# Where the sorting of batch 3's keys sits among the second dense layers of batch 2

## The chip, the cores and the metric

The kernel runs on one NeuronCore of a Trainium2 chip. The metric is the device time of one execution in microseconds (us), lower is better; each kernel is run several times and the median is compared.

The engines of the core each work through their own list of instructions in order. TensorE (PE) multiplies matrices and writes its results to PSUM; VectorE (DVE) and ScalarE (ACT) take results out of PSUM and compute on them; GpSimd (POOL) and SyncE (SP) here mostly start transfers (DMAs). An engine waits for another by a semaphore. "PEld" in the profile is TensorE's loading of the stationary operand, which can overlap its multiplying.

## The reference

For 4 batches of 8 heads, 768 positions and head size 64, a small 8x8 matrix per head is normalised five times over rows and columns (`P`). The 8 blocks (of 96 positions) of the keys and of the values are mixed with it, each block of queries attends to its mixed block, and the result goes through a two-layer dense network:

```python
k_sorted = np.einsum('bhij,bhjcd->bhicd', P, k_b)     # "sorting" the keys
v_sorted = np.einsum('bhij,bhjcd->bhicd', P, v_b)     # and the values
scores = scale * np.matmul(q_b, k_sb.transpose(0, 1, 2, 4, 3))
attn = softmax(scores)                                # within one block
x = np.matmul(attn, v_sb)                             # 3072 tokens x 512
h = x @ w_in                                          # 512 -> 2048
r = np.maximum(h, 0.0)
out = (s * (r * r) + b) @ w_out                       # 2048 -> 512
```

## The kernel before

The work is cut into 8 tiles `t` of 384 tokens, two per batch (`t` = 2b and 2b+1). A tile passes through these pieces:

- `k_piece(b, c0, nc2, nb, eng)` (multiplied at L294) sorts a part of a batch's keys. The pieces of this text, `K(3, c0, 16, eng)`, load 16 pairs of key columns from `kb` one after the other as the stationary operand, multiply each with the mixing matrix into one PSUM buffer `tk`, and copy this to `ks` with four casts, on DVE (`eng` "v", L238) or ACT (`eng` "s", L240). Three pieces with `c0` = 0, 32, 64 make a batch.
- `S2(t, hp)` is two calls of `s_piece`: scores (L375) into PSUM buffers `sc`, and their exponentials on ACT into `at` (L378). It needs the sorted keys `ks` of its batch.
- `P2(t, hp)` is two calls of `p_piece`: attention times sorted values `vs` (L402) into PSUM buffers `pv`, then a reciprocal and a multiplication on DVE into `x` (L406, L407).
- `T(t)` is `x_turn`: a transposing DMA on SP's queue from `x` to `xt` (L452).
- `ffn1(t)` (L473) multiplies by `w_in`; ACT takes the positive part (L477) and DVE squares it into `gt` (L478).
- `ffn2(t)` (L516) multiplies by `w_out`: three row groups of 16 matmuls into a PSUM buffer `ops`; DVE scales it, adds the bias (L490) and SP stores it (L492).

All orders are written by hand: the program's order is each engine's order. To fill TensorE's list evenly, `ffn1` and `ffn2` take a `Queue` of attention pieces for later tiles. `ffn2` calls the queue after every fourth matmul, so `ffn2(2)` and `ffn2(3)` together have 24 slots, numbered 0 to 23 below; the queue of the change has 24 entries, one per slot (`nothing` is an empty one).

PSUM is given out in turn from two pools. The one that matters here, `psa`, has three buffers, used in rotation by `tk`, `sc`, `pv` and `hps` (the result of `ffn1`). A piece that takes a buffer waits until its last reader has finished.

Ahead of this queue, POOL starts the transfers of batch 2 and 3 (L664 to L668), once the queries of batch 2 have been transposed:

```python
nc.gpsimd.tensor_copy(out=gate2, in_=QT[2][0:1, NHP - 1, S - 1:S])
v_read(2, nc.gpsimd)       # sorted values of batch 2, two DMAs (vs<-dv, L361)
load_k(*brows(3))          # keys of batch 3, one DMA (kb<-in_k_dram, L97)
v_read(3, nc.gpsimd)       # sorted values of batch 3, two DMAs
load_q(3)                  # queries of batch 3, six DMAs (L84)
```

Slot 22 of the queue, `q_turn(3)`, transposes those queries on SP's queue. The sorted keys and the turned queries of batch 3 are first read by `S2(6, 0)`, in `ffn2(4)`, after `ffn1(4)` and `ffn1(5)`.

Of the kernel before, what the change touches and what calls it, by code (L numbers as in the profile page):

```python
# [18 lines left out]
def kernel(  # L19
# [58 lines left out]
    def load_q(b, part=slice(0, 128)):  # L78


        if b > 1:
            qr[b] = qrp.tile([128, TQ, H, D], BF, tag="qr", name=f"qr{b}")
            for t in range(TQ):
                nc.gpsimd.dma_start(  # L84
                    out=qr[b][:, t],
                    in_=q[b][:, t * 128:(t + 1) * 128, :].rearrange("h p d -> p h d"))
            return
        if b not in qr:
            qr[b] = qrp.tile([128, H, TQ, D], BF, tag="qr", name=f"qr{b}")
        nc.gpsimd.dma_start(  # L90
            out=qr[b][part].rearrange("p h t d -> p h (t d)"),
            in_=q[b].rearrange("h (p t) d -> p h (t d)", t=TQ)[part])

    def load_k(rows, prow, n=1):
        for c0 in range(0, BLK, BLK // n):
            cs = slice(c0, c0 + BLK // n)
            nc.gpsimd.dma_start(out=kb[prow, cs, :], in_=kraw[rows, cs, :])  # L97
# [4 lines left out]
    def brows(b):  # L102
        return slice(b * 64, (b + 1) * 64), slice((b % 2) * 64, (b % 2) * 64 + 64)
# [157 lines left out]
    def q_piece(b, hp0, eng):  # L261

        if hp0 == 0:
            QT[b] = qtp.tile([128, NHP, S], BF, tag="qt", name=f"qt{b}")
        ps = psa.tile([128, 2, 1024], BF, tag="a", name="tq")
        for i in range(2):
            for t in range(TQ):
                for e in range(2):
                    nc.tensor.transpose(
                        out=ps[e * 64:(e + 1) * 64, i, t * 128:(t + 1) * 128],  # L270
                        in_=qr[b][:, 2 * (hp0 + i) + e, t, :], identity=ident)
        evac(QT[b][:, hp0:hp0 + 2, :].rearrange("q a (p t) -> q a p t", t=TQ),
             ps[:, :, 0:S].rearrange("q a (t p) -> q a p t", t=TQ), eng)

    def q_turn(b):

        QT[b] = qtp.tile([128, NHP, S], BF, tag="qt", name=f"qt{b}")
        for t in range(TQ):
            nc.sync.dma_start(out=QT[b][:, :, t * 128:(t + 1) * 128],
                              in_=qr[b][:, t].rearrange("p h d -> p (h d)"), transpose=True)  # L280

    def k_piece(b, c0, nc2, nb, eng):

        pr = brows(b)[1] if nb == 1 else slice(0, 128)
        rhs = (pd1[pr] if b < 2 else pd2[pr, b - 2]).rearrange("p e m i -> p (e m i)")
        if nc2 * nb > 8:
            ps = psa.tile([128, nc2, nb * 64], FP, tag="a", name="tk")  # L290
        else:
            ps = psb.tile([128, nc2, nb * 64], FP, tag="b", name="tk")
        for c in range(nc2):
            nc.tensor.matmul(out=ps[:, c, :],  # L294
                             lhsT=kb[pr, c0 + 2 * c:c0 + 2 * c + 2, :].rearrange("p c d -> p (c d)"),
                             rhs=rhs, start=True, stop=True)
        g0 = (b % 2) * 32

        def half(cp):
            if b == 0:  # L300
                cs = slice(c0 + cp, c0 + 2 * nc2, 2)
            else:
                cs = slice(cp * (BLK // 2) + c0 // 2, cp * (BLK // 2) + c0 // 2 + nc2)
            for e in range(2):
                evac(ks[e * 64:(e + 1) * 64, g0:g0 + nb * 32, cs].rearrange(
                         "p (b g) c -> p b g c", b=nb),
                     ps[cp * 64:(cp + 1) * 64].rearrange(
                         "p c (b e g) -> p e b g c", b=nb, e=2)[:, e], eng)

        half(0)  # L310
        return lambda: half(1)
# [54 lines left out]
    def s_piece(t, hp):  # L366

        b, half = divmod(t, 2)
        g0 = (b % 2) * 32 + hp * NB + half * HB
        sc = psa.tile([BLK, 2, 512], FP, tag="a", name="sc")  # L370
        for n in range(HB):
            for e in range(2):
                pr = slice(e * 64, (e + 1) * 64)
                q0 = (half * HB + n) * BLK
                nc.tensor.matmul(out=sc[:, e, n * BLK:(n + 1) * BLK], lhsT=ks[pr, g0 + n, :],  # L375
                                 rhs=QT[b][pr, hp, q0:q0 + BLK], start=True, stop=True)
        at = atp.tile([BLK, 2, TG], BF, tag="at", name="at")
        nc.scalar.activation(out=at, in_=sc[:, :, 0:TG], func=AF.Exp, scale=scale)  # L378
        AT[t, hp] = at

    def p_piece(t, hp, n0=0, nn=HB):

        b, half = divmod(t, 2)
        at = AT[t, hp]
        if t not in X:
            X[t] = xp.tile([BLK, HB, d_model], BF, tag="x", name="x")
        x = X[t]
        atf = at.rearrange("p e t -> p (e t)")
        if nn < HB:
            p1 = psb.tile([128, 512], FP, tag="b", name="pv")  # L390
            pv = [p1[:, e * nn * VW:(e + 1) * nn * VW] for e in range(2)]
            pvv = p1[0:BLK, 0:2 * nn * VW].rearrange("p (e n w) -> p e n w", e=2, w=VW)
        else:
            p2 = psa.tile([128, 2, 512], FP, tag="a", name="pv")
            pv = [p2[:, 0], p2[:, 1]]
            pvv = p2[0:BLK, :, 0:nn * VW].rearrange("p e (n w) -> p e n w", w=VW)
        for e in range(2):
            for n in range(n0, n0 + nn):
                c0 = (e * HB + n) * BLK
                m = 128 if c0 + 128 <= 2 * TG else BLK  # L400
                gi = e * 32 + hp * NB + half * HB + n
                nc.tensor.matmul(out=pv[e][0:m, (n - n0) * VW:(n - n0 + 1) * VW],  # L402
                                 lhsT=atf[:, c0:c0 + m],
                                 rhs=VS[b][:, gi, :], start=True, stop=True)
        rec = rtp.tile([BLK, 2, HB], FP, tag="rec", name="rec")
        nc.vector.reciprocal(out=rec[:, :, 0:nn], in_=pvv[:, :, :, D])  # L406
        nc.vector.tensor_tensor(  # L407
            out=x[:, n0:n0 + nn, hp * 128:(hp + 1) * 128].rearrange("p n (e d) -> p e n d", e=2),
            in0=pvv[:, :, :, 0:D],
            in1=rec[:, :, 0:nn].unsqueeze(3).broadcast_to([BLK, 2, nn, D]), op=ALU.mult)  # L410
# [38 lines left out]
    def x_turn(t):  # L449

        XT[t] = xtp.tile([128, HB * NHP, BLK], BF, tag="xt", name="xt")
        nc.sync.dma_start(out=XT[t], in_=X[t].rearrange("p n m -> p (n m)"), transpose=True)  # L452
# [87 lines left out]
    def seq(*fs):  # L540
        def run():
            for f in fs:
                f()
        return run

    def S2(t, hp):
        return lambda: (s_piece(t, hp), s_piece(t, hp + 1))

    def P2(t, hp):
        return lambda: (p_piece(t, hp), p_piece(t, hp + 1))  # L550

    def T(t):
        return lambda: x_turn(t)

    def attn(t):
        return [S2(t, 0), nothing, P2(t, 0), S2(t, 2), nothing, P2(t, 2), nothing, T(t)]
# [77 lines left out]
    def csums(f0, f1):  # L634
        for f in range(f0, f1):
            if f == 1:
                nc.gpsimd.tensor_tensor(out=csum, in0=wo_at(0), in1=wo_at(1), op=ALU.add)
            elif f > 1:
# [9 lines left out]
    qu = Queue([nothing, lambda: q_piece(1, 2, "v")]  # L648
               + [lambda c0=c0: k_piece(1, c0, 16, 1, "vsv"[c0 // 32])() for c0 in range(0, BLK, 32)]
               + [seq(lambda: load_q(2), lambda: load_k(*brows(2)), bias_piece), V2[0], S2(2, 0), V2[1], S2(2, 2), V2[2], V2[3],  # L650
                  P2(2, 0), V2[4], P2(2, 2), V2[5], S2(3, 0),
                  T(2), P2(3, 0), S2(3, 2), nothing, P2(3, 2), T(3), lambda: q_turn(2)], 24)
# [3 lines left out]
    def K(b, c0, nc2, eng):  # L656
        return lambda: k_piece(b, c0, nc2, 1, eng)()

    qu = Queue([nothing if i % 2 else K(2, i * 8, 8, "vs"[i // 2 % 2]) for i in range(12)]
               + [nothing] * 4, 16)  # L660
# [5 lines left out]
    load_k(*brows(3))  # L666
    v_read(3, nc.gpsimd)
    load_q(3)  # L668
    qu = Queue([S2(4, 0), K(3, 0, 16, "s"), nothing, P2(4, 0), nothing, S2(4, 2), nothing,
                K(3, 32, 16, "s"), P2(4, 2), nothing, T(4), K(3, 64, 16, "v"), S2(5, 0), nothing,  # L670
                nothing, P2(5, 0), nothing, S2(5, 2), nothing, P2(5, 2), nothing, T(5),
                lambda: q_turn(3), nothing], 24)
    ffn2(2, qu)
    ffn2(3, qu)
# [2 lines left out]
    qu = Queue(attn(6) + attn(7), 24)  # L677
# [36 lines left out]
```

## Time and profile before

| | |
|---|---|
| time, median of 13 runs | 237.28 us |
| lowest and highest of these runs | 236.15 and 238.92 us |
| the profiled execution's own time | 238.71 us |
| span of the profile | 237.0 us |
| mean granted TensorE clock | 0.964 |
| TensorE busy with matmuls | 226.9 us, 96% of the span |
| VectorE, ScalarE, GpSimd busy | 121.9, 111.9, 48.4 us |

The profile shows one execution; its times count from the start of its span. The busy share of an engine is an average over stages. Which stage is held up by what is read from the waits, and from the list of instructions in order of time. The granted clock is the share of full speed at which TensorE was allowed to run.

### The profile page before, as it was taken

Reading aid. Unit: us, or ns where it says so; the run is one execution under the profiler, and the core shown is the slowest. Engines: PE = TensorE matmul, PEld = TensorE weight load, DVE = VectorE, ACT = ScalarE, POOL = GpSimd, SP = SyncE. Lnnn points to the kernel's source line nnn. Section 1 sums busy time; section 2 is a strip of 40 time slices with the busy share of each in tenths; the row PEclk is TensorE's granted clock in tenths of the full one; section 3 lists DMA queues with packets and bytes.
Section 4 is the critical chain, followed back from the end, with each engine's and each line's share of the span. In section 5 each row is a group of like instructions: output and inputs, shape, how many; then the busy total and the mean of one; then the engine's idle time right before and its main releaser. Section 6 shows DMA issues by size and latency. Waiting matters only on the chain.

```text
span 237.0 us, 4847 instructions
## 1 busy us (share of the span) xinstructions
PE 226.9 (96%) x2036; PEld 137.3 (58%) x2036; DVE 121.9 (51%) x257; ACT 111.9 (47%) x164; POOL 48.4 (20%) x62
## 2 busy tenths in 40 slices
PE   8969999999999999999789999999999999999994
PEld 5769897765544555555345455665554556554442
DVE  4768556638992646666322745434352544342221
ACT  6158479675157451778635321566422225660000
POOL 7820000399991000059210000000000000000000
PEclk9975599999999999999979999999999999999999
DMA  5799999998699995539999815630024142001122
GB/s 91 116 203 211 230 192 205 228 225 177 88 117 182 297 273 131 121 62 123 156 104 162 173 44 117 86 89 1 3 85 103 58 116 39 3 0 44 59 77 89
DMA packets 46694, 28.90 MB, mean 122 GB/s; under 512 B 35920, under 2 KB 41040, under 8 KB 46160
## 3 DMA queue, kind: packets, MB, share of 16 engines
q0 software_dynamic: 18800, 15.21, 49.1%
q1 hardware_dynamic: 27728, 13.32, 24.5%
q8 instruction: 16, 0.26, 0.5%
q10 hardware_dynamic: 144, 0.07, 0.1%
q14 instruction: 6, 0.05, 0.1%
HBM read 29.63 MB, written 8.65 MB: 162 GB/s over the span
## 4 chain that ended last, share of the span: by engine, by line
PE 63%; issue 15%; DMA 10%; POOL 8%; ACT 2%; DVE 0%; POOLq 0%
PE hps L473 25%; PE ops L516 25%; DMA kb<-in_k_dram 5%; DMA qr<-in_q_dram 5%; POOL csum L639 4%; PE pv L402 3%; PE sc L375 2%; POOL qr L84 2%; PE tv L320 2%; PE ops L501 1%; ACT ks L240 1%; PE wp L182 1%; PE tq L254 1%; PE tk L294 1%; PE tv L336 1%
## 5 line engine op out<-in xcount | busy, mean ns | idle before, releaser
L473 PE MATMUL hps<-xt,wi 128*128 128x384 bf16 (+1 forms) x576 | 88.1, 309 | 0.3 <-ACT rt L477 0.3
L516 PE MATMUL ops<-wo,gt 128*128 128x512 bf16 x368 | 87.8, 383 | 0.4 <-DVE ot L490 0.4
L477 ACT ACTIVATE rt<-hps 128x768 bf16<-128x768 f32 (+1 forms) x72 | 53.2, 741 | 45.0 <-PE hps L473 44.2
L473 PEld LDWEIGHTS <-wi 128*128 128x128 bf16 x576 | 53.7, 98 | 30.3 <-issue 1.3
L478 DVE TENSOR_TENSOR gt<-rt 128x768 bf16<-128x768 bf16 (+1 forms) x72 | 41.2, 575 | 47.1 <-ACT rt L477 46.7
L516 PEld LDWEIGHTS <-gt 128*128 128x128 bf16 x368 | 34.1, 99 | 38.2 <-issue 2.0
L490 DVE SCALAR_TENSOR_TENSOR ot<-ops,s_bc,bias 128x512 f32<-128x512 f32 x23 | 17.1, 749 | 44.4 <-PE ops L516 44.3
L378 ACT ACTIVATE at<-sc 96x768 bf16<-96x768 f32 x32 | 24.4, 804 | 29.2 <-PE sc L375 29.1
L407 DVE TENSOR_TENSOR x<-pv,rec 96x512 bf16<-96x512 f32 (+1 forms) x36 | 22.6, 627 | 1.3
L240 ACT CAST ks<-tk 64x512 bf16<-64x512 f32 (+1 forms) x32 | 16.0, 501 | 8.6 <-PE tk L294 8.3
L238 DVE CAST ks<-tk 64x512 bf16<-64x512 f32 (+1 forms) x32 | 18.1, 565 | 2.0 <-PE tk L294 1.5
L639 POOL TENSOR_TENSOR csum<-csum,wo 128x512 f32<-128x512 f32 x14 | 17.6, 1255 | 1.0
L402 PEld LDWEIGHTS <-at 96*128 96x128 bf16 (+1 forms) x256 | 12.5, 106 | 4.1 <-issue 0.6
L182 PE MATMUL wp<-zt 128*128 128x256 bf16 x86 | 13.4, 319 | 1.1 <-DVE warm L113 1.1
L402 PE MATMUL pv<-vs,at 96*128 96x66 bf16 (+1 forms) x256 | 13.4, 202 | 0.1
L240 ACT CAST vn<-tv 128x512 bf16<-128x512 f32 (+1 forms) x12 | 9.4, 799 | 7.2 <-PE tv L350 6.7
L375 PEld LDWEIGHTS <-ks 64*96 64x96 bf16 x256 | 8.5, 128 | 5.8 <-issue 5.1
L84 POOL DMA_DIRECT2D qr<-in_q_dram x12 | 10.6, 912 | 5.4 <-DMA kb<-in_k_dram 3.0
L406 DVE RECIPROCAL rec<-pv 96x8 f32<-96x8 f32 (+1 forms) x36 | 6.9, 192 | 8.7 <-PE pv L402 8.6
L182 PEld LDWEIGHTS <-zt 128*128 128x128 bf16 x86 | 9.2, 113 | 2.9 <-DVE warm L113 1.1
L375 PE MATMUL sc<-qt,ks 64*96 64x96 bf16 x256 | 10.8, 219 | 0.0
L294 PEld LDWEIGHTS <-kb 64*128 64x128 bf16 x192 | 6.7, 98 | 6.7 <-issue 4.0
(73 smaller groups left out, 98.8 us busy)
## 6 DMA issues: line engine op xcount, KB each, us to landing
out_dram<-ot SPq DMA_DIRECT2D x23, 256.0 KB, 2.3
kb<-in_k_dram POOLq DMA_DIRECT2D x4, 768.0 KB, 11.8
vb<-in_v_dram POOLq DMA_DIRECT2D x4, 768.0 KB, 19.8
wi<-in_moe_w_in_dram POOLq DMA_DIRECT2D x2, 1024.0 KB, 20.2
wo<-in_moe_w_out_dram POOLq DMA_DIRECT2D x2, 1024.0 KB, 32.5
qr<-in_q_dram POOLq DMA_DIRECT2D x12, 128.0 KB, 9.9
dv<-vn SPq DMA_DIRECT2D x6, 256.0 KB, 7.6
vs<-dv POOLq DMA_DIRECT2D x4, 384.0 KB, 13.2
```

Of the source, the lines that this page charges most:

```text
L182: nc.tensor.matmul(out=wp, lhsT=zt[:, 0:128], rhs=zt, start=True, stop=True)
L238: nc.vector.tensor_copy(out=out, in_=in_)
L240: nc.scalar.copy(out=out, in_=in_)
L375: nc.tensor.matmul(out=sc[:, e, n * BLK:(n + 1) * BLK], lhsT=ks[pr, g0 + n, :], rhs=QT[b][pr, hp, q0:q0 + BLK], start=True, stop=True)
L378: nc.scalar.activation(out=at, in_=sc[:, :, 0:TG], func=AF.Exp, scale=scale)
L402: nc.tensor.matmul(out=pv[e][0:m, (n - n0) * VW:(n - n0 + 1) * VW], lhsT=atf[:, c0:c0 + m], rhs=VS[b][:, gi, :], start=True, stop=True)
L407: nc.vector.tensor_tensor(out=x[:, n0:n0 + nn, hp * 128:(hp + 1) * 128].rearrange("p n (e d) -> p e n d", e=2), in0=pvv[:, :, :, 0:D], in1 ...
L473: nc.tensor.matmul(out=hps[:, f, 0:nt], lhsT=wi_at(hp, f0 + f), rhs=xt_at(t, hp, n0, nn), start=(hp == 0), stop=(hp == NHP - 1))
L477: nc.scalar.activation(out=rt[:, :, 0:nt], in_=hps[:, :, 0:nt], func=AF.Relu)
L478: nc.vector.tensor_tensor(out=gt[:, f0:f0 + 2, c0:c0 + nt], in0=rt[:, :, 0:nt], in1=rt[:, :, 0:nt], op=ALU.mult)
L516: nc.tensor.matmul(out=ops, lhsT=gt[:, f, m * 128:(m + 1) * 128], rhs=wo_at(f), start=(f == 0), stop=(f == NF - 1))
L639: nc.gpsimd.tensor_tensor(out=csum, in0=csum, in1=wo_at(f), op=ALU.add)
```

## The change

The three pieces that sort batch 3's keys leave slots 1, 7 and 11 and go to slots 11, 14 and 20 of the same queue. The piece in slot 11 is still evacuated by VectorE, the two others by ScalarE. All other entries keep their slots.

```diff
-    qu = Queue([S2(4, 0), K(3, 0, 16, "s"), nothing, P2(4, 0), nothing, S2(4, 2), nothing,
-                K(3, 32, 16, "s"), P2(4, 2), nothing, T(4), K(3, 64, 16, "v"), S2(5, 0), nothing,
-                nothing, P2(5, 0), nothing, S2(5, 2), nothing, P2(5, 2), nothing, T(5),
+    qu = Queue([S2(4, 0), nothing, nothing, P2(4, 0), nothing, S2(4, 2), nothing, nothing,
+                P2(4, 2), nothing, T(4), K(3, 0, 16, "v"), S2(5, 0), nothing, K(3, 32, 16, "s"),
+                P2(5, 0), nothing, S2(5, 2), nothing, P2(5, 2), K(3, 64, 16, "s"), T(5),
                 lambda: q_turn(3), nothing], 24)
```

## The prediction, made before the changed kernel was run

> **What bounds the kernel now.** I read the page first: the span, the busy times, the slices.
>
> ```profile
> span 237.0 us, 4847 instructions
> PE 226.9 (96%) x2036; PEld 137.3 (58%) x2036; DVE 121.9 (51%) x257; ACT 111.9 (47%) x164; POOL 48.4 (20%) x62
> PE   8969999999999999999789999999999999999994
> PEclk9975599999999999999979999999999999999999
> ```
>
> TensorE bounds it: no other engine is busy for much over half of the span. A slice is 5.9 us. Apart from the start and the end, the PE row is below 9 only in slices 19 and 20 (112.6 to 124.4 us), and the clock row is below 9 after the start only in slice 20. This is the stage of the edited queue. I then asked for TensorE's waits. From 30 to 117 us they come to 0.7 us, from 126 us to the end to none. For 98 to 150 us they are:
>
> ```profile
> PEld L294 <- DMA kb<-in_k_dram: 2.7, 1, 2.7
> PE tk L294 <- DMA kb<-in_k_dram: 2.2, 1, 2.2
> ```
>
> Columns: total, times, longest. One wait of 2.2 us, for the keys of batch 3, by the first matmul of `K(3, 0)`. The timeline shows what it follows and what stands behind it:
>
> ```profile
> 115.68 0.56 PE L375 MATMUL sc<-qt,ks 64*96 64x96 bf16 x16
> 116.17 1.04 PE L516 MATMUL ops<-wo,gt 128*128 128x512 bf16 x4
> 119.39 0.64 PE L294 MATMUL tk<-pd,kb 64*128 64x64 bf16 x16 [2.19 <-DMA kb<-in_k_dram]
> 119.96 2.60 PE L516 MATMUL ops<-wo,gt 128*128 128x512 bf16 x8
> 122.35 1.14 PE L402 MATMUL pv<-vs,at 96*128 96x66 bf16 x16
> ```
>
> Slot 0 (`S2(4, 0)`), four dense matmuls, then the wait in slot 1; everything in later slots is queued behind it. The stage table shows a second price, the granted clock (after the engines, before the DMA share):
>
> ```profile
> 118.00:119.00 1.00, 0.00 (x0) 0.00 (x0) 0.00 (x0) 0.00 (x0) 0.00 (x0) 1.00 1.02 107
> 121.00:122.00 1.00, 1.00 (x4) 0.38 (x3) 0.00 (x0) 0.98 (x3) 0.00 (x0) 0.51 0.94 86
> 123.00:124.00 1.00, 1.00 (x11) 0.58 (x9) 0.97 (x3) 0.00 (x0) 0.00 (x0) 0.50 1.12 127
> 124.00:125.00 1.00, 1.00 (x5) 0.41 (x4) 0.97 (x3) 0.00 (x0) 0.00 (x0) 0.78 2.84 111
> ```
>
> From 121.0 to 124.4 us, just after the idle stretch, TensorE ran at half clock. The chain of waits, in order of time, gives what that cost:
>
> ```profile
> 119.39 0.64 PE tk L294 x16
> 120.03 2.53 PE ops L516 x8
> 122.56 0.93 PE pv L402 x16
> 123.49 2.26 PE ops L516 x8
> 125.75 0.49 PE sc L375 x16
> 126.23 1.83 PE ops L516 x8
> 128.07 0.57 PE tk L294 x16
> ...
> 129.61 0.54 PE pv L402 x16
> ```
>
> The same pieces at full clock follow in the list: 8 dense matmuls 1.83 us, a `P2` 0.54 us.
>
> **The change, step by step.**
>
> *Removed: the wait.* The keys were asked for at 106.56 us and landed 12.8 us later, at 119.35 us. Their first user moves from slot 1 (about 117.2 us) to slot 11, which I place below at 127.6 us: 8.2 us of slack. Gain 2.19 us, and 0.07 us for the slow first piece (0.64 against 0.57).
>
> *Removed: the half clock, if the idle stretch caused it.* (2.53 - 1.83) + (0.93 - 0.54) + (2.26 - 1.83) = 1.52 us. [...] The trace speaks otherwise: half clock for 3.4 us right behind that gap, none anywhere else after the first 30 us, though equal key pieces without a wait run at 128 and 132.7 us. I take the trace: 1.52 us for the profiled execution. [...]
>
> *Moved: three key pieces.* Each is 16 weight loads, 16 matmuls and four casts, and issues no DMA; POOL's and SP's lists keep their order, and nothing is moved past a transfer. TensorE's work is the same: three times 0.57 us. The number of places where dense matmuls are interrupted stays 11 too. The piece in slot 11 stays VectorE's; its four casts (2.78 us) are there before and after, so VectorE's list is unchanged. ScalarE's two groups of casts (2.35 us each) move from behind the exponentials of slots 0 and 5 to behind those of slots 12 and 17.
>
> *The stage rebuilt.* With the chain's pieces from 116.17 us: 12 dense matmuls 2.70, `P2` 0.54, 8 dense 1.83, `S2` 0.49, 12 dense 2.70, `P2` 0.54, 12 dense 2.59: slot 11 at 127.56. Then key piece 0.57, 4 dense 0.97, `S2` 0.49, 8 dense 1.83, key piece 0.57, 4 dense 0.97, `P2` 0.54, 8 dense 1.73, `S2` 0.49, 8 dense 1.83, `P2` 0.53, 4 dense 0.97, key piece 0.57, 12 dense 2.59: `ffn1(4)` begins at 142.2 instead of 146.03 us, 3.8 us earlier. Step by step it was 2.19 + 0.07 + 1.52 = 3.8. Both agree.
>
> *What is late next.* `P2(4, 0)` in slot 3 is now the first to need a transfer, at 116.17 + 2.70 = 118.9 us. The two transfers of batch 2's values were started at 103.85 and 105.22 us. The transfer table has the first alone, then both (median of two):
>
> ```profile
> vs<-dv POOLq DMA_DIRECT2D x1, 384.0 KB, 7.7
> ...
> vs<-dv POOLq DMA_DIRECT2D x2, 384.0 KB, 9.0
> ```
>
> So the second took 2 x 9.0 - 7.7 = 10.3 us and landed at 115.5 us, 3.4 us ahead of need. It is started before the keys on the same queue and landed 3.8 us before them: an execution with slower transfers delays both. The exponentials that `P2(4, 0)` needs end at 117.6 us. No wait: 0.
>
> *New tight places*, all on the rotation of three PSUM buffers. The piece in slot 14 takes the buffer of the piece in slot 11: VectorE finished that 3.48 us after its first matmul (132.74 to 136.22 in the timeline of before), TensorE comes back 3.86 us after it (0.57 + 0.97 + 0.49 + 1.83). Margin 0.4 us; if a delay eats it, TensorE waits that much, say up to 0.5 us. `S2(5, 2)` at 135.2 needs the slot-14 buffer, whose casts end at 131.4 + 0.67 + 2.35 = 134.4: margin 0.8. The last casts begin 0.67 us after 139.05 and end at 142.1, while ScalarE is needed by the first result of `ffn1(4)` at 142.2 + 1.34 = 143.5: margin 1.5, and the shortfall beyond it would be the cost. Together 0, bounds -0.1 and +0.8. The sorted keys are first read at 168.5 - 3.8 = 164.7 us, over 22 us later. The transposed queries too: their last transfer was issued at 119.63, the six had a median of 17.6 us to landing, and the transposes go at about 142 us; should they wait, SP's list waits with them, with the first store of `ffn2(3)`'s last rows behind, not TensorE.
>
> *After the stage.* From 126 us on TensorE has no wait; what is won here is kept to the end. Tail and start are untouched.
>
> *Sum.* 238.71 - 3.8 = 234.9 us for the profiled execution. It lay 1.43 us above the median. If that excess is the half clock, the median run loses 2.2 us only, and 237.28 - 2.2 = 235.1 results: the same place. If the excess came from the start, the median run gains all of it: 237.28 - 3.8 = 233.5 us. I take 234.9.
>
> **The rivals.**
>
> *The half clock stays* (about one in eight): it has another cause, or another short gap brings it. Then 2.3 us are won: 238.71 - 2.3 = 236.4 on the profiled execution, 235.0 from the median. [...] Against it: the place of the dip.
>
> *The wait is mostly moved, or typical runs hardly have it* (about one in twelve): the lowest run, 236.15, is 2.56 us below the profiled one, so some executions may have little to win; with the tight PSUM places costing 0.8, 236.2 to 238. Against: then another 2.5 us of variation would have to sit at the start.
>
> *Slower: TensorE waits for batch 2's values in slot 3* (one in twenty). The wait decides the other way if those land 2 us after need, at 120.9 instead of 115.5: 234.9 + 2.0 + 1.5 for a half-clock stretch = 238.4, 0.5% above the median; at 3 us, 239.4. For it: this is the first transfer met[...]. Against it: in the trace the keys come 3.8 us behind the values, so a run with the values 2 us late for slot 3 would have had the keys at 124.8 us, a wait of some 7.6 us in the kernel before, and no run was beyond 238.92.
>
> *The change does nothing* (within the second rival): excluded as far as order goes, since TensorE's list differs only in these 48 matmuls and their weight loads.
>
> **How the numbers follow.** Full gain 0.75, half clock stays 0.12, little or none 0.08, slower 0.05. About 0.5% (1.2 us) is what a measurement of this kernel can tell from no change: faster means below 236.1 us. The first case and nearly all of the second lie there, 0.87; the third is the same, 0.08; the last slower, 0.05. The range goes from the full gain off the median, 233.5 and a tenth, to the second rival's 236.4.
>
> **What would show it.** Right: no TensorE wait on `kb`, no granted clock below 1.00 between 30 us and the end, slot 3's `P2` at about 118.9 us, the first `ffn1(4)` matmul 26.0 us after the end of slot 0's scores instead of 29.9. Wrong: a wait of the first `pv` matmul for `vs`, of `tk` or `sc` for DVE or ACT of a microsecond, or a half-clock stretch that remains without the gap.

## The result, and the profile after

The changed kernel took 235.02 us (median of 11 runs, 234.56 to 235.20). The kernel before, its new runs pooled with the earlier ones, took 237.71 us (48 runs, 236.00 to 239.06). The ratio is 0.9886, 95% interval 0.9861 to 0.9911: 1.1% faster. Forecast were 234.9 us and 233.4 to 236.4.

The profiled execution after took 235.37 us with a span of 233.7 us. Its page, the lines that answer to those of before:

```profile
span 233.7 us, 4849 instructions
PE 225.8 (97%) x2036; PEld 137.1 (59%) x2036; DVE 122.0 (52%) x257; ACT 111.9 (48%) x164; POOL 48.4 (21%) x62
PE   8969999999999999999999999999999999999994
PEclk9995599999999999999999999999999999999999
```

The dent in slices 19 and 20 is gone from the PE row, and the 7 in slice 20 from the clock row; VectorE, ScalarE and GpSimd are busy as long as before to 0.1 us; TensorE's busy time falls by 1.1 us: about 1.5 us less here, where its matmuls no longer run at half clock, and about 0.5 us more at the start (see below). TensorE's waits from 30 us to the end are now:

```profile
PE ops L516 <- DVE ot L490: 0.4, 1, 0.4
PE hps L473 <- ACT rt L477: 0.3, 1, 0.3
```

The wait for `kb` is not in the list. These two were there before. The chain of waits, in order of time (start, duration), through the edited queue:

```profile
116.31 0.49 PE sc L375 x16
116.80 2.70 PE ops L516 x12
119.50 0.53 PE pv L402 x16
120.03 1.73 PE ops L516 x8
...
125.48 2.59 PE ops L516 x12
128.07 0.57 PE tk L294 x16
...
131.93 0.57 PE tk L294 x16
...
139.46 0.57 PE tk L294 x16
140.03 2.70 PE ops L516 x12
142.72 5.36 PE hps L473 x33
```

It is TensorE all the way, each piece at its full-clock duration. From the end of slot 0's scores (116.80) to the first matmul of `ffn1(4)` (142.72) it takes 25.9 us, against 29.9 before. The spans differ by 3.3 and not by the 4.0 of this stage because this execution reached it later: its scores ended at 116.80 instead of 116.17 us, after a half-clock stretch at the start that is as long as in the trace of before (13.65 us) but ends later, at 30.0 instead of 28.9 us (the granted clock of 29.0 to 29.5 us is 0.50 here, 1.00 there).

### The profile page after: what moved, and what is told of

It reads as the page before. It is cut to its first block, busy times and chain, and to the rows that moved or that the text cites. A ratio compares the mean times of both kernels' runs of the same rounds, so it can differ in the third digit from the quotient of the medians.

```text
span 233.7 us, 4849 instructions
## 1 busy us (share of the span) xinstructions
PE 225.8 (97%) x2036; PEld 137.1 (59%) x2036; DVE 122.0 (52%) x257; ACT 111.9 (48%) x164; POOL 48.4 (21%) x62
## 4 chain that ended last, share of the span: by engine, by line
PE 83%; DVE 7%; DMA 5%; ACT 2%; issue 1%; POOL 0%; POOLq 0%
PE hps L473 35%; PE ops L516 32%; DMA qr<-in_q_dram 5%; PE pv L402 4%; PE sc L375 3%; DVE gt L478 2%; DVE ks L238 2%; PE tv L320 2%; PE tk L294 2%; PE ops L501 2%; ACT ks L240 1%; PE tv L350 1%; PE wp L182 1%; PE tq L254 1%; PE tv L336 1%
## 5 line engine op out<-in xcount | busy, mean ns | idle before, releaser
L516 PE MATMUL ops<-wo,gt 128*128 128x512 bf16 x368 | 86.5, 379 | 0.4 <-DVE ot L490 0.4
L378 ACT ACTIVATE at<-sc 96x768 bf16<-96x768 f32 x32 | 24.4, 804 | 29.5 <-PE sc L375 29.3
L182 PE MATMUL wp<-zt 128*128 128x256 bf16 x86 | 14.0, 328 | 1.1 <-DVE warm L113 1.1
```

The lines of the kernel that those rows point to most:

```text
L182: nc.tensor.matmul(out=wp, lhsT=zt[:, 0:128], rhs=zt, start=True, stop=True)
L516: nc.tensor.matmul(out=ops, lhsT=gt[:, f, m * 128:(m + 1) * 128], rhs=wo_at(f), start=(f == 0), stop=(f == NF - 1))
```

## The experiments

Theory: the gain is a wait of TensorE for the keys' transfer, and a stretch of half clock that this idle gap brings in a part of the executions. Rivals: the two other pieces, moved off ScalarE and the PSUM rotation in the first half, are part of the gain; the half clock has another cause than the gap. All edits below are to the kernel before.

### Only the first piece, three slots later

```diff
-    qu = Queue([S2(4, 0), K(3, 0, 16, "s"), nothing, P2(4, 0), nothing, S2(4, 2), nothing,
+    qu = Queue([S2(4, 0), nothing, nothing, P2(4, 0), K(3, 0, 16, "s"), S2(4, 2), nothing,
```

> Only the first key piece moves, from slot 1 to slot 4 (about 120.4 us, 1 us after the keys land at 119.4); the two others stay in slots 7 and 11. Theory (the gain is the wait and the half clock that follows it): the whole gain, 235.0 us (234.6 to 235.4), no TensorE wait on kb, narrow spread as in the changed kernel. Rival (ScalarE's or the PSUM buffers' relief by moving the others matters): 235.5 to 236.5. Rival (the half clock has another cause): about 236.4 in runs with it.

Measured: 234.93 us (5 runs, 234.62 to 235.12), ratio 0.9874 (0.9839 to 0.9909), no wait on `kb`. In the timeline the piece starts where the matmuls before it end:

```profile
119.54 1.03 PE L516 MATMUL ops<-wo,gt 128*128 128x512 bf16 x4
120.50 0.64 PE L294 MATMUL tk<-pd,kb 64*128 64x64 bf16 x16
```

So the whole gain comes from moving one piece past the landing of its keys. That the three stand in the second half of the queue is not needed for it.

### The first piece left in slot 1, a later one moved

```diff
-                K(3, 32, 16, "s"), P2(4, 2), nothing, T(4), K(3, 64, 16, "v"), S2(5, 0), nothing,
-                nothing, P2(5, 0), nothing, S2(5, 2), nothing, P2(5, 2), nothing, T(5),
+                nothing, P2(4, 2), nothing, T(4), K(3, 64, 16, "v"), S2(5, 0), nothing,
+                K(3, 32, 16, "s"), P2(5, 0), nothing, S2(5, 2), nothing, P2(5, 2), nothing, T(5),
```

> The first key piece stays in slot 1; the two others stand late, in slots 11 and 14 (VectorE and ScalarE). Theory: no gain, 237.7 us with the spread of the kernel before (236.0 to 239.1), wait of 2.2 us on kb in the trace. Rival (relief of ScalarE and PSUM by the late pieces is part of the gain): 236.5 to 237.2.

Of the two, only `K(3, 32)` changes its place, from slot 7 to 14; `K(3, 64)` had slot 11 before as well, and its further move to slot 20 is not in this run. Measured: 237.94 us (22 runs, 236.38 to 238.77), ratio 1.0003 (0.9982 to 1.0025). No gain: taking this piece, which ScalarE evacuates, out of the first half is worth nothing that shows. That the moves of both together add nothing is seen from the run before this one: with them the time is 235.02 us, without them 234.93. The one profiled execution happened to be the fastest, and it shows the wait alone:

```profile
PE tk L294 <- DMA kb<-in_k_dram: 1.6, 1, 1.6
```

```profile
116.00:118.00 2.00, 1.08 (x10) 0.31 (x4) 0.48 (x3) 1.48 (x2) 0.00 (x0) 1.00 1.09 143
118.00:120.00 2.00, 1.29 (x20) 0.89 (x21) 0.00 (x0) 0.60 (x2) 0.88 (x1) 1.00 0.94 82
120.00:122.00 2.00, 2.00 (x25) 1.17 (x24) 0.78 (x2) 1.71 (x3) 0.00 (x0) 1.00 1.03 96
122.00:124.00 2.00, 2.00 (x24) 1.02 (x23) 1.57 (x4) 0.21 (x1) 0.00 (x0) 1.00 1.38 123
```

In this stage table the first number after the length is TensorE's busy time, and the clock stands after the five engines: 1.00 throughout, though TensorE was idle for 1.6 us. This execution took 236.38 us, the profiled one of the kernel before, with its 2.19 us of idle time and its half clock, 238.71.

### The gap filled, the wait left

```diff
-    def k_piece(b, c0, nc2, nb, eng):
+    def k_piece(b, c0, nc2, nb, eng, fill=0):
...
+        for _ in range(fill):
+            nc.tensor.matmul(out=ps[:, 0:4, :].rearrange("p c d -> p (c d)"), lhsT=zt[:, 0:128],
+                             rhs=zt, start=True, stop=True)
         for c in range(nc2):
             nc.tensor.matmul(out=ps[:, c, :],
...
-    qu = Queue([S2(4, 0), K(3, 0, 16, "s"), nothing, P2(4, 0), nothing, S2(4, 2), nothing,
+    qu = Queue([S2(4, 0), lambda: k_piece(3, 0, 16, 1, "s", 16)(), nothing, P2(4, 0), nothing, S2(4, 2), nothing,
```

> The kernel before, with 16 multiplications of zeros (128x256) put ahead of the first key piece in slot 1, into the buffer that the piece then overwrites: about 1.8 us of TensorE work inside the 2.2 us wait. The first piece starts when the keys land as before. Theory (the idle gap brings the half clock): the wait stays paid, the half clock goes: 235.0 + 2.2 = 237.2 us, granted clock about 0.971 in every run, spread under 0.8 us. Rival (the half clock comes from something else in this stage): as before, 236.0 to 239.1 us, clock down to 0.964 in some runs.

Measured: 236.86 us (22 runs, 236.27 to 237.59), ratio 0.9976 (0.9955 to 0.9998); the spread of 1.3 us is wider than the 0.8 us forecast. The timeline shows the filled gap, with 0.2 us of it left (the added lines shift line numbers by three):

```profile
117.56 1.91 PE L294 MATMUL tk<-zt 128*128 128x256 bf16 x16
119.70 0.64 PE L297 MATMUL tk<-pd,kb 64*128 64x64 bf16 x16 [0.23 <-DMA kb<-in_k_dram]
120.27 1.90 PE L519 MATMUL ops<-wo,gt 128*128 128x512 bf16 x8
```

The 8 dense matmuls behind it take 1.90 us, not 2.60.

The runs tell more than the median. The 48 runs of the kernel before fall into two groups of 24, 236.00 to 237.52 (median 236.9) and 237.91 to 239.06 (median 238.4), with nothing between 237.52 and 237.91. With the gap filled none of 22 runs lies in the upper group. So idle TensorE time in this place, and not this stage's other work, brings the upper group. Nor is it a later landing of the keys, which the filling would not have helped.

That the upper group is the half clock rests on its size, the two medians being 1.5 us apart as the term read off one trace (1.52 us), and on the traces: the execution at 238.71 us has the stretch, those at 236.38 (above) and 237.37 us (this run) do not. The mean clock of a run doesn't tell the groups apart, because the half-clock stretch at the start differs too (13.65 us in the traces of before and after; about 10.2 us in the one with the first piece ahead of the queue, by its granted clock of 0.88 over 14 to 18 us and 0.68 over 26 to 28 us): in the 81 further runs of the kernel before that stand beside these experiments it is 0.961 to 0.971 from 237.9 us up and 0.968 to 0.978 below. These runs show the same two groups, about half in each, though four of them lie between 237.52 and 237.91.

The lower group and the filled kernel give the price of the wait alone: 236.9 - 235.0 = 1.9 us and 236.86 - 235.02 = 1.8 us. The profiled execution, with 2.19 us, waited longer than that.

### The first piece one slot later, and one slot earlier

```diff
-    qu = Queue([S2(4, 0), K(3, 0, 16, "s"), nothing, P2(4, 0), nothing, S2(4, 2), nothing,
+    qu = Queue([S2(4, 0), nothing, K(3, 0, 16, "s"), P2(4, 0), nothing, S2(4, 2), nothing,
```

> Only the first key piece moves, from slot 1 to slot 2, four dense matmuls (0.9 us) later. Theory: the wait shrinks from 2.2 to 1.3 us, so 236.3 us if the half clock no longer comes, 236.3 to 237.9 with a spread if it still comes in some runs. Rival (the half clock does not depend on the gap): the same spread as before, 0.9 us lower, median 236.8.

Measured: 235.67 us (6 runs, 235.00 to 236.03), ratio 0.9903 (0.9870 to 0.9936), and in the trace of the fastest of them:

```profile
PE tk L294 <- DMA kb<-in_k_dram: 0.4, 1, 0.4
```

The wait shrinks as the piece moves. It is smaller than forecast because that started from the 2.2 us of one long wait; 1.9 less 0.9 would be 1.0, and 0.65 was measured. A part of this difference is the start: four of the six runs have a mean clock of 0.978, and in the trace of one of them the half-clock stretch there ends earlier, at about 27.1 us (granted clock 0.72 over 26 to 28 us) against 28.9 in the kernel before. Against runs of the changed kernel with a like clock, 0.8 us (0.976 and up) and 0.9 to 1.0 us (0.969 to 0.971) remain. No run shows an upper group.

```diff
-    qu = Queue([S2(4, 0), K(3, 0, 16, "s"), nothing, P2(4, 0), nothing, S2(4, 2), nothing,
+    qu = Queue([seq(S2(4, 0), K(3, 0, 16, "s")), nothing, nothing, P2(4, 0), nothing, S2(4, 2), nothing,
```

> The first key piece moves one slot earlier, into slot 0 directly behind the scores of S2(4, 0): the same landing of the keys, but no dense matmuls between, so the gap grows by 0.9 us to 2.5 to 3.1 us. Theory (wait paid one to one, and a half-clock stretch whose chance grows with the gap): 235.0 + 2.5 to 3.1, plus about 1.5 us in most or all runs, median about 239.2, few runs below 238.3. [...] Rival (half clock independent of the gap): as before plus 0.9, two groups of about equal size at 237.5 and 239.2.

Measured: 238.39 us (22 runs, 237.26 to 239.57), ratio 1.0037 (1.0016 to 1.0059). The wait grew, and the profiled execution had the half clock behind it:

```profile
PE tk L294 <- DMA kb<-in_k_dram: 3.1, 1, 3.1
```

```profile
120.00:122.00 2.00, 2.00 (x8) 0.82 (x7) 0.00 (x0) 1.97 (x4) 0.27 (x1) 0.66 0.96 88
122.00:124.00 2.00, 2.00 (x7) 0.63 (x6) 0.00 (x0) 0.18 (x1) 0.00 (x0) 0.50 1.14 124
```

But 10 of the 22 runs lie at 237.26 to 237.94, in the place of a wait without half clock. The other 12 lie at 238.27 to 239.57. The forecast that most or all runs would have the half clock failed: a gap of 3.1 us in the trace, against 2.19, did not bring it surely.

### What decides about the half clock

In four of the traces so far TensorE waited over 1.5 us for a transfer. The gaps are read from the timelines, that is the time without a matmul, the half clock from the granted clock in the stage tables:

| trace | gap, us | length | half clock |
|---|---|---|---|
| before | 117.21 to 119.39 | 2.19 us | 121.0 to 124.4 us |
| piece in slot 0 | 116.07 to 119.16 | 3.09 us | 120.6 to 124.0 us |
| later piece moved | 117.08 to 118.71 | 1.63 us | none, 1.00 from 112 to 126 us |
| keys early (below) | 91.51 to 94.41 | 2.90 us | none, by pace: 16 dense matmuls from 96.15 us took 2.77 us, as in the kernel before from 93.00 us |

Half clock followed two of the four gaps. In both traces it began 1.5 to 1.6 us after the gap's end and lasted 3.4 us. The 2.90 us gap of the last row was longer than that of the first and brought none, so these traces are not ordered by the length of the gap. That a gap longer than all of them would bring the half clock in every run was the author's estimate, and the next run tested it.

```diff
+    K(3, 0, 16, "s")()
-    qu = Queue([S2(4, 0), K(3, 0, 16, "s"), nothing, P2(4, 0), nothing, S2(4, 2), nothing,
+    qu = Queue([S2(4, 0), nothing, nothing, P2(4, 0), nothing, S2(4, 2), nothing,
```

> The first key piece moves still further ahead, to the end of the dense first layer, before the first matmul of the second layer: the wait for the same landing grows to 3.8 to 4.5 us. [...]every run gets the half clock and no lower group remains: 235.0 + 3.8 to 4.5 + 1.5 = 240.3 to 241.0, lowest run above 239.6. Rival (half clock by chance, independent of the gap): two groups of about equal size, 238.8 to 239.5 and 240.4 to 241. [...]

Measured: 240.92 us (6 runs, 240.22 to 242.19; on another chip, where the kernel before took 237.16 us in 11 runs), ratio 1.0166 (1.0130 to 1.0202). No lower group. In the trace:

```profile
PE tk L294 <- DMA kb<-in_k_dram: 4.1, 1, 4.1
```

```profile
116.00:118.00 2.00, 0.00 (x0) 0.00 (x0) 0.27 (x2) 0.00 (x0) 0.25 (x1) 1.00 1.00 141
118.00:120.00 2.00, 1.33 (x19) 0.85 (x20) 0.00 (x0) 0.64 (x2) 0.87 (x1) 0.86 1.09 90
120.00:122.00 2.00, 2.00 (x20) 0.92 (x19) 0.00 (x0) 1.95 (x4) 0.00 (x0) 0.50 0.96 92
122.00:124.00 2.00, 2.00 (x9) 0.80 (x8) 0.00 (x0) 1.23 (x2) 0.00 (x0) 0.79 1.44 124
```

The gap ran from 114.55 to 118.67 us, and the clock fell at about 119.4 us (the mean of 0.86 over 118 to 120 us places it) and rose at about 122.8 us (0.79 over 122 to 124 us): 3.4 us of half clock once more. Two runs above 242 us are beyond the forecast; they and a third, at 241.16 us, have the lowest mean clock (0.957), and no trace was taken of them.

The idle time alone does not tell whether half clock follows, however. TensorE also stops at the end of the program. First the kernel with the later piece moved, then the one with the gap filled, each with the stretch that holds its last matmuls and the time behind it:

```profile
229.79:233.20 3.41, 1.55 (x21) 1.17 (x18) 0.97 (x2) 0.00 (x0) 0.00 (x0) 1.00 0.35 121
233.20:234.60 1.40, 0.00 (x0) 0.00 (x0) 0.00 (x0) 0.00 (x0) 0.00 (x0) 1.00 0.00 0
```

```profile
231.22:234.63 3.41, 1.11 (x18) 0.88 (x15) 0.97 (x2) 0.00 (x0) 0.00 (x0) 1.00 0.23 77
234.65:235.60 0.95, 0.00 (x0) 0.00 (x0) 0.00 (x0) 0.00 (x0) 0.00 (x0) 0.50 0.00 0
```

In the first, TensorE is idle for 1.86 us and then for 1.40, and the granted clock is 1.00 throughout; in the second it is idle for 2.30 us, and the clock behind them is 0.50. In the trace of the kernel before no matmul runs in the last 3 us, from 234 to 237 us, and the granted clock is 1.00 to the end.

What decides beside the idle time was not shown. Nor is the share of runs explained: 24 of 48 lie in the upper group of the kernel before, with 2.19 us of gap in its trace, and 12 of 22 in that of slot 0, with 3.09 us. The two groups would fit a cause that changes from run to run; this is the author's estimate and was not seen run by run.

### The keys earlier instead of the piece later

```diff
+    load_k(*brows(3))
     gate2 = sk.tile([1, 1], BF)
     nc.gpsimd.tensor_copy(out=gate2, in_=QT[2][0:1, NHP - 1, S - 1:S])
     v_read(2, nc.gpsimd)
-    load_k(*brows(3))
     v_read(3, nc.gpsimd)
```

> The kernel before with all pieces in their old slots, but the transfer of batch 3's keys is started right after that of batch 2's keys (about 71 us) and not behind the turned queries (106 us). Theory (only the date of the keys matters): no wait in slot 1, no half clock, 235.0 us (234.5 to 235.4), as in the changed kernel. Rival (the early transfer collides with the stores and reads of the stage at 70 to 100 us): no wait in slot 1, but new TensorE waits between 70 and 105 us, 235.5 to 238. Rival (the order of the pieces matters beside the keys): 235.5 to 236.5 without any wait for a transfer.

Measured: 239.51 us (6 runs, 237.99 to 241.46), ratio 1.0101 (1.0062 to 1.0141): slower. The wait in slot 1 is gone, and another has come:

```profile
PE hps L473 <- DMA xt<-x: 2.9, 1, 2.9
```

```profile
89.62 1.89 PE L516 MATMUL ops<-wo,gt 128*128 128x512 bf16 x8
94.41 1.47 PE L473 MATMUL hps<-xt,wi 128*128 128x384 bf16 x8 [2.90 <-DMA xt<-x]
...
119.32 1.04 PE L516 MATMUL ops<-wo,gt 128*128 128x512 bf16 x4
120.29 0.64 PE L294 MATMUL tk<-pd,kb 64*128 64x64 bf16 x16
```

The key piece follows its predecessor at 120.29 us without a wait, but `ffn1(2)` begins 2.9 us late, because the turned rows `xt` of its tile are late. SP's queue shows where that began: its waits from 76 to 100 us hold one that the kernel before does not have,

```profile
SPq L354 <- DMA dv<-vn: 2.8, 1, 2.8
```

The last store of sorted values waited 2.8 us for an earlier one to land (median time to landing of these six stores 11.4 us, 7.6 before). The transpose `T(2)` stands behind it on SP's queue: it started at 86.92 instead of 84.09 us and took 7.4 us instead of 4.8. The rival of a collision held, and cost more than its 238 us at most. The profiled execution, without a half-clock stretch, was the fastest of the six; the mean clock of the five others, 0.957 to 0.964 against its 0.971, would fit half-clock stretches behind the new gap; that was not shown, since no trace was taken of them. Of the two ways to bring keys and piece together, moving only TensorE's work cost nothing here.

No version here is faster than the changed kernel: with the first piece alone in slot 4 the time is the same within the runs' spread (234.93 and 235.02).

## Why the prediction was right

- *The wait.* Right. It is gone: TensorE reaches the first key piece at 128.07 us, and the keys were there by 119.67 us, when a transfer of POOL that waits for them was started. Moving that piece alone brings all of the gain; with it left in slot 1, moving a later piece brings none.
- *The half clock.* Right in cause and size: 1.52 us by the trace, 1.5 us between the two groups of runs, none with the gap filled. To count it from the trace of before was the choice that mattered: without it the gain forecast would have been 2.3 us (2.19 + 0.07) and not 3.8. A gap of 2.19 us had half clock behind it in that trace, and the upper group of the runs is half of them.
- *Which execution stands for the median.* Half right. The prediction left open whether the profiled execution's excess of 1.43 us was the half clock. It was mostly that: 24 of 48 runs lie in the upper group, so the median lies between two groups, 236.9 and 238.4, and moves with the draw (237.28 in 13 runs, 237.71 in 48). The term mis-sized was the wait: 2.19 us in that execution, 1.9 us typically. The total fell on the forecast because the changed kernel is nearly the same in all runs: 0.64 us between its lowest and highest, against 3.06 before. That it did so to 0.1 us is partly luck: for the profiled execution 234.9 us was the sum, but it took 235.37, having reached the stage 0.6 us later than the one of before, and no term of the sum was for the start.
- *The stage rebuilt.* 26.0 us from the end of slot 0's scores were forecast, 25.9 measured; it had all its pieces from the chain of before at full clock.
- *What is late next.* Nothing, as forecast. `P2(4, 0)` started at 119.50 us in the chain, 2.70 us after the scores, with no wait for `vs`.
- *The tight PSUM places.* Right, and as tight as said. The timeline after has VectorE's casts and the piece that takes their buffer:

```profile
128.78 2.78 DVE L238 CAST ks<-tk 64x512 bf16<-64x512 f32 x4
131.86 0.64 PE L294 MATMUL tk<-pd,kb 64*128 64x64 bf16 x16
132.54 2.36 ACT L240 CAST ks<-tk 64x512 bf16<-64x512 f32 x4 [1.07 <-PE tk L294]
135.67 0.56 PE L375 MATMUL sc<-qt,ks 64*96 64x96 bf16 x16
```

  The casts end at 131.56 and the piece starts at 131.86: 0.3 us were left (0.4 forecast). ScalarE's end at 134.90, the scores come at 135.67: 0.8, as forecast. The last casts end at 142.42, and ScalarE takes the first result of `ffn1(4)` at 144.06: 1.6 us (1.5 forecast).
- *The rivals.* That the half clock stays is excluded by the clock row and by the narrow spread. That typical runs hardly wait is excluded: the lower group still loses 1.9 us. The wait for the values did not come, and in no trace here did a `P2` wait for them.

## What to carry to other kernels

In a list of instructions that runs in order, look for the first user of each transfer and ask whether work that needs nothing from it can stand in front; here one piece moved by three slots gave the whole 1.1%. Price an idle gap of the matmul engine by what follows it too: here the half clock behind it cost 1.5 us where the gap itself cost 1.9 us. When the runs of a kernel fall into two groups, find out in which of them the profiled execution lies before its numbers are set against a median.

## What the runs showed of the hardware that was not expected

- Half clock for about 3.4 us followed gaps of 2.19, 3.09 and 4.12 us in three traces, while gaps of 1.63 and 2.90 us in two others had none behind them. At the end of the program one trace kept full clock through 3.3 us of idle time, another had half clock behind 2.3 us.
- Multiplications of zeros, 16 of 128x256 in 1.91 us, in place of the gap left the granted clock at 1.00 from 112 to 126 us of the trace: the upper group of runs vanished (0 of 22 against 24 of 48) while the wait for the keys stayed paid.
- A transfer of 768 KB started 35 us earlier, in a stage that looked covered, went with slower stores (median 11.4 us to landing instead of 7.6) and, behind them on SP's queue, a transpose that started at 86.92 instead of 84.09 us and took 7.4 instead of 4.8 us, until TensorE waited 2.9 us for it.
